# A fused attention and gated-MLP block on one core: the prologue's work is dealt out anew among the engines, and its order changed

## The chip, the cores and the metric

The kernel runs on one core of a Trainium2 chip. The metric is the device time of one execution in microseconds (us). Four compute engines take part: TensorE (PE in the profile), VectorE (DVE), ScalarE (ACT) and GpSimd (POOL); SyncE (SP) only issues DMAs. DMAs issued by SP run on a queue that the profile calls hardware_dynamic, those issued by GpSimd on one that it calls software_dynamic.

## The reference, cut to what matters

```python
# x: (1, 2048, 512); wqkv: (512, 1536); 32 heads of 16; F = 1792, Fh = 896
xn  = layernorm(x)                                  # eps 1e-5, no scale or shift
q, k, v = split_heads(xn @ wqkv)
A = softmax(q k^T / 4) v   ... @ wo                 # attention over all 2048 tokens
z = gelu(xn @ w_in);  z1 = z[..., :Fh];  z2 = layernorm(z[..., Fh:])
B = (z1 * (w_sp z2 + b_sp)) @ w_out                 # gMLP, w_sp mixes the 2048 tokens
out = x + A + B
```

All is fp32. The kernel gets fp32 accuracy from TensorE's fp32r format by splitting both operands of a product into a high part (rounded to fp32r) and a low part (what is left), and adding three products: high x high, low x high, high x low (`mm3`, lines 236 to 238).

## The kernel before, in words

**Tiling.** The 2048 tokens are 4 groups of 512, each of 4 tiles of 128 tokens. The width of 512 is 4 chunks of 128 (`ND` = 4). The 32 heads are taken in 16 pairs (`p`); q and k of four pairs come from one piece of weights, `m` = 0 to 3.

**Prologue** (before the line `steady.append(True)`). For each group g:

- `load_x(g)`: two DMAs by SP bring the group's tokens into the tiles `x{g}_0` and `x{g}_2`, two token tiles each.
- `norm_x(g)`: layernorm. DVE makes mean and variance of each tile (L318, L319), ACT the square root (L321), DVE the reciprocal and the shift (L322, L323), and then each tile of 128 x 512 is scaled and shifted in place (L327). With `parts` = 2 this goes by halves of two tiles. It is a generator, so its caller can run it in steps between other work.
- `turn_x(g)`: TensorE transposes the 16 blocks of 128 x 128 (L333), four to a PSUM bank; ACT copies each bank to the high half of `xnT{g}_{c}` (L71 in the profile, the line of the helper) and DVE subtracts to get the low half (L233).
- `qk_first(g)`: q and k of the first four head pairs for the group, each 12 matmuls of 128 x 512 (L236 to L238), then a split by ACT and DVE into the tile `qkhl`, and stores by SP to DRAM scratch (`qscr`, `kscr`): for q and for k one store of 512 KB and one of 256 KB.
- `load_stacks(0, ...)`: four loads of 96 KB by SP from that scratch into `qst0` and `kst0`, the stacked operands of the first head pair. SP works in order: a load that waits for its store to land holds what is queued behind it.
- `v_tile(t)`: V of one token tile, 12 matmuls (L236 to L238), evicted by ACT. Four of the 16 tiles (`EARLY` = 4) are done here, one a group; they use group 0's tokens. The weights of V (`wv0` to `wv3`) lie in `qst1` and `kst1`, which are free at that time.

Then `store(xscr[g][c], xnT[g, c])` writes the 16 tiles of the turned tokens, 512 KB each, to DRAM scratch, for the later work that reads them again. The code has these after the loop, and in the prologue `store` issues on GpSimd's queue (L155).

**Weights.** `begin` loads a piece of weights by SP in raw fp32; with `early` given, a second DMA, by GpSimd (L253), loads the same bytes straight into the high half (so that no copy is needed), and `end` then subtracts on DVE (L259). Without `early`, `end` lets GpSimd copy (L261) and subtract (L262). In the steady part other weights are split by GpSimd in the same way (L282, L284).

**Constants.** `cscr` is a row of ones in DRAM; `init_rows(a)` copies it to four rows of `kst[a]`, which carry the softmax shift into the scores' product. `init_rows(0)` belongs to the prologue and `init_rows(1)` to the first third of the first head pairs' work. `braw` and `bhl` hold the spatial bias `b_sp`.

**Order of the work.** Everything is written out in program order (`manual_schedule`): each engine takes its instructions in the order in which the code issues them, and waits by semaphores for operands and free buffers. After the prologue a planner, with costs and due times written in the code, interleaves the scores and their maxima (L1109 before the change), the dense products of the rest of V, q, k and the MLP (L1154), the scores for the softmax (L1095) and the products with V (L1192). After the prologue TensorE's first work is 48 dense matmuls for the next V tiles, and then the first maxima: products of `kst0` and `qst0`, of which the fourth pair of products needs the fourth group's k. DVE reduces them (L811).

Of the kernel before, what the change touches and what calls it, by code (L numbers as in the profile page):

```python
# [16 lines left out]
P = 128  # L17
# [36 lines left out]
def fused_block(ctx, tc, x, wqkv, wo, w_in, w_spT, b_sp, w_out, out):  # L54
# [66 lines left out]
    def raw(t):  # L121
        return t.bitcast(F32) if t.dtype == F32R else t

    def move(dst, src):
        nc.sync.dma_start(raw(dst), raw(src))
# [93 lines left out]
    def t512(nm):  # L219
        return big.tile([P, 512], F32, tag="t512", name=nm, bufs=4)  # L220
# [86 lines left out]
    def norm_x(g, parts=1):  # L307


        mv = sm.tile([P, 4, 2], F32, tag="mv", name=f"mv{g}", bufs=2)  # L310
        rs = sm.tile([P, 2, 4], F32, tag="rs", name=f"rs{g}", bufs=2)
        k = 4 // parts
        for a in range(parts):
            tiles = range(a * k, (a + 1) * k)
            sl = slice(a * k, (a + 1) * k)
            for i in tiles:
                st = sm.tile([P, 6], F32, tag="bst", name=f"bst{g}_{i}", bufs=4)
                nc.vector.bn_stats(st, xs[g, i])  # L318
                nc.vector.bn_aggr(mv[:, i, :], st)  # L319
            yield  # L320
            nc.scalar.activation(rs[:, 0, sl], mv[:, sl, 1], AF.Sqrt, bias=epst)  # L321
            nc.vector.reciprocal(rs[:, 0, sl], rs[:, 0, sl])  # L322
            nc.vector.scalar_tensor_tensor(rs[:, 1, sl], mv[:, sl, 0], -1.0, rs[:, 0, sl], ALU.mult, ALU.mult)  # L323
            for i in tiles:
                if i % 4 == 2:
                    yield
                nc.scalar.activation(xs[g, i], xs[g, i], AF.Identity, bias=rs[:, 1, i:i + 1], scale=rs[:, 0, i:i + 1])  # L327

    def turn_x(g):
        for c in range(ND):  # L330
# [635 lines left out]
        for _ in gen:  # L966
            pass

    def init_rows(a):

        for j in range(2):
            row = 64 * j + KS
            for r in range(2):
                nc.gpsimd.dma_start(raw(kst[a])[row + r:row + r + 1, :], cscr[0:1, :])

    engines = {mybir.EngineType.PE, mybir.EngineType.Activation, mybir.EngineType.DVE, mybir.EngineType.Pool, mybir.EngineType.SP}
    with tc.manual_schedule(engines=engines):
        load_x(0)
        w0 = [piece(f"wqk0_{a}") for a in range(2)]
        w0r = [begin(*qk_weights(0, a), early=w0[a]) for a in range(2)]  # L980
        load_x(1)
        ones = t512("ones")
        nc.vector.memset(ones[0:32, 0:P], 1.0)
        wv, wvr = [], []
        for c in range(ND):
            t = (qst, kst)[c // 2][1].rearrange("p (b a f) -> p b a f", b=2, a=2)[:, c % 2]
            wv.append(t)
            wvr.append(begin(f"wv{c}", wqkv[c * P:(c + 1) * P, 2 * D:3 * D], 512, early=t))
        nc.gpsimd.dma_start(cscr.rearrange("o (a b) -> (o a) b", b=P), ones[0:16, 0:P])
        nc.gpsimd.memset(vhead[:, :, :, DH:], 1.0)  # L990
        nc.gpsimd.memset(vall[:, NT * H * (DH + 1):], 0.0)
        for r in (0, 64):
            nc.vector.tensor_copy(onesr[r:r + 2, :], ones[0:2, 0:P])
        run(norm_x(0, 2))
        load_x(2)
        for r, t in zip(w0r, w0):
            end(r, t, True)
        turn_x(0)
        load_x(3)
        init_rows(0)  # L1000
        for r, t in zip(wvr, wv):
            end(r, t, True)
        norm = norm_x(1, 2)
        for g in range(NG):
            for _ in qk_first(g, w0):
                if g == 0:
                    next(norm, 0)
            load_stacks(0, slice(g * 512, (g + 1) * 512))
            for t in range(EARLY * g // NG, EARLY * (g + 1) // NG):
                v_tile(t, wv)  # L1010
            if g + 1 < NG:
                for _ in norm:
                    pass
                turn_x(g + 1)
                if g + 2 < NG:
                    norm = norm_x(g + 2)
                    next(norm)
        for g in range(NG):
            for c in range(ND):
                store(xscr[g][c], xnT[g, c])  # L1020
        steady.append(True)
        braw = t512("braw")[0:16, 0:P]
        bhl = hilo("bhl")[0:16, :, 0:P]
        move(braw, b_sp)
        nc.vector.tensor_copy(bhl[:, 0, :], braw)
        nc.vector.tensor_sub(bhl[:, 1, :], braw, bhl[:, 0, :].bitcast(F32))
        for a in range(2):
            move(bsplit[a:a + 1, :], bhl[:, a, :])
        T.update(P=0.0, A=0.0, D=0.0, G=0.0)
        room["big"] = RING - 16 + EARLY  # L1030
        prepare(wq, [((m, a), *qk_weights(m, a)) for m in (1, 2, 3) for a in range(2)])
# [50 lines left out]
        def scores():  # L1082
            nonlocal n_st
            p, c, kt = order[n_st]
            if n_st == 22:
                init_rows(1)
            i = n_st % 64
            if p + 1 < NP and stacks[0] <= p and i >= (3 if p else 20) and (not owed[0] or i >= LATE):
                stacks[0] = p + 1
                load_stacks(p + 1)  # L1090
            turn_to("R")
            k = take("s")
            for j in range(2):
                rows = slice(64 * j, 64 * j + KS + 2)
                nc.tensor.matmul(sl[k][:, j, :], kst[p % 2][rows, kt * P:(kt + 1) * P], qst[p % 2][rows, c * 512:(c + 1) * 512], start=True, stop=True)  # L1095
            T["P"] += SLOT
            spawn(exp(n_st, k), 1, T["P"] + 0.22)
            stpos[n_st] = pe
            n_st += 1
# [203 lines left out]
```

## Time and profile before

| | |
|---|---|
| time before, median of 3 runs | 1884.51 us (1882.85 to 1885.61) |
| the profiled execution's own time | 1888.93 us |
| its span in the trace | 1887.1 us |
| mean granted TensorE clock | 0.989 |
| TensorE busy | 1825.1 us of the span (97%) |
| VectorE, ScalarE, GpSimd busy | 1444.7, 1225.3, 690.7 us |
| TensorE's first matmul, first one after the prologue | 8.06, 74.40 us |

Times in rows of the trace are microseconds from the start of the span. A row of the timeline reads: start, length, engine, line, operation, out<-in, count, and in brackets the idle time before it with what ended it. A row of a group reads: line, engine, operation, names, shapes, count, then busy time and mean of one in ns, then idle time before and what ended it. Engine names with a q (SPq) are the engine's DMA issues.

### The profile page before, as it was taken

What the parts mean: (1) busy time and instruction counts of PE and PEld (TensorE: products, weight loads), DVE (VectorE), ACT (ScalarE), POOL (GpSimd) and SP (SyncE); (2) the same over time, 40 slices, a digit from 0 to 9 for tenths busy, and PEclk for the clock granted to TensorE, in tenths of its full rate; (3) what the DMA queues carried; (4) which work ended last, traced back from release to release, by engine and by line L of the source; (5) the groups of instructions that cost most, each with busy time, mean ns of one, the idle gap of its engine ahead of it and who ended that gap; (6) DMA issues with size and microseconds to landing.
All of it is one profiled execution on the core that took longest, in us unless ns stands there. A gap on an engine that the chain in (4) does not pass through costs nothing.

```text
span 1887.1 us, 38105 instructions
## 1 busy us (share of the span) xinstructions
PE 1825.1 (97%) x14812; PEld 1109.3 (59%) x14812; DVE 1444.7 (77%) x1677; ACT 1225.3 (65%) x1338; POOL 690.7 (37%) x797
## 2 busy tenths in 40 slices
PE   6899999999998999999999999999999999999998
PEld 5665656566554656566655656565656565556554
DVE  5577878888876878778777877787778777878873
ACT  4247777888775777666656666666666665656555
POOL 2202142687886878800171217000722140002110
PEclk9899999999998999999999999999999999999999
DMA  9505573444455353474677657463787576456342
GB/s 329 208 3 170 203 225 111 98 137 118 133 160 160 129 130 110 141 167 119 158 201 194 165 142 227 133 148 103 219 194 160 161 201 145 124 140 174 116 129 92
DMA packets 208109, 291.47 MB, mean 154 GB/s; under 512 B 36008, under 2 KB 107368, under 8 KB 205048
## 3 DMA queue, kind: packets, MB, share of 16 engines
q1 hardware_dynamic: 197944, 258.03, 50.6%
q0 software_dynamic: 9984, 31.01, 4.8%
q8 instruction: 116, 1.90, 0.4%
q14 instruction: 65, 0.53, 0.1%
HBM read 186.98 MB, written 101.98 MB: 153 GB/s over the span
## 4 chain that ended last, share of the span: by engine, by line
PE 84%; DMA 4%; DVE 4%; POOL 4%; issue 2%; ACT 2%; SPq 0%; DVEq 0%; POOLq 0%; ACTq 0%
PE dps L1154 33%; PE sl L1192 22%; PE sl L1095 13%; PE sl L1109 12%; DVE mm L811 3%; DMA mscr<-ms 1%; PE dps L1168 1%; POOL wsp L284 1%; ACT pf L71 1%; DMA wqk<-in_wqkv 1%; PE sl L236 0%; PE sl L237 0%; DMA qst<-mscr 0%; PE sl L238 0%; ACT x L327 0%
## 5 line engine op out<-in xcount | busy, mean ns | idle before, releaser
L811 DVE TENSOR_REDUCE mm<-sl 128x2 f32<-128x1024 f32 x1024 | 1226.2, 1223 | 184.0 <-PE sl L1109 178.3
L71 ACT ACTIVATE pf<-sl 128x1024 f32<-128x1024 f32 x1024 | 1042.9, 1027 | 356.6 <-PE sl L1095 315.4
L1192 PE MATMUL sl<-pf,vall 128*32 128x512 f32 x4096 | 467.3, 597 | 0.0
L1095 PE MATMUL sl<-qst,kst 50*128 50x512 f32 x2048 | 441.4, 421 | 13.0 <-DVE mm L811 2.9
L1154 PE MATMUL dps<-wsp,zs 64*128 64x512 f32 x2688 | 441.4, 393 | 3.1 <-DMA zs<-z2scr 3.1
L1109 PE MATMUL sl<-kst,qst 48*128 48x512 f32 x2048 | 428.1, 408 | 7.2 <-DVE mm L811 3.5
L1095 PEld LDWEIGHTS sl<-qst,kst 50*128 50x128 f32 x2048 | 197.6, 185 | 223.8 <-issue 85.7
L1154 PEld LDWEIGHTS dps<-wsp,zs 64*128 64x128 f32 x2688 | 266.8, 187 | 41.5 <-DMA zs<-z2scr 3.7
L1192 PEld LDWEIGHTS sl<-pf,vall 128*32 128x32 f32 x4096 | 120.3, 110 | 270.6 <-issue 241.1
L1109 PEld LDWEIGHTS sl<-kst,qst 48*128 48x128 f32 x2048 | 197.6, 186 | 113.5 <-ACT pf L71 54.6
L1212 DVE TENSOR_TENSOR e<-sl,e 128x512 f32<-128x512 f32 x64 | 44.3, 692 | 174.3 <-PE sl L1192 133.8
L720 POOL TENSOR_TENSOR hhl<-z1i,hhl 128x512 fp32r<-128x512 f32 x28 | 35.8, 1290 | 332.3 <-ACT hhl L71 332.3
L71 ACT ACTIVATE e<-sl 128x512 f32<-128x512 f32 x64 | 38.3, 599 | 176.5 <-PE sl L1192 159.9
L1154 PE MATMUL dps<-w,xt 64*128 64x448 f32 x768 | 110.9, 369 | 2.3 <-ACT z L71 0.4
L1154 PE MATMUL dps<-wout,hp 64*128 64x512 f32 x672 | 111.5, 393 | 0.0
L858 POOL TENSOR_TENSOR ob<-ob 128x512 f32<-128x512 f32 (+1 forms) x16 | 20.6, 1288 | 181.9 <-DMA ob<-rscr 181.9
L1154 PEld LDWEIGHTS dps<-w,xt 64*128 64x128 f32 x768 | 73.9, 186 | 17.1 <-issue 8.0
L420 POOL TENSOR_TENSOR qkhl<-qr,qkhl 128x512 fp32r<-128x512 f32 x24 | 30.4, 1285 | 115.2 <-ACT qkhl L71 93.7
L1154 PEld LDWEIGHTS dps<-wout,hp 64*128 64x128 f32 x672 | 65.5, 187 | 9.1
L854 POOL TENSOR_TENSOR ob<-ob 128x512 f32<-128x512 f32 (+1 forms) x16 | 21.0, 1312 | 96.8 <-DMA ob<-escr 96.8
L1154 PE MATMUL dps<-xnT,wqk 64*128 64x512 f32 x288 | 47.4, 396 | 1.1 <-ACT vall L71 0.4
L1154 PE MATMUL dps<-wo,op 64*128 64x512 f32 x288 | 47.5, 407 | 0.6
(279 smaller groups left out, 1629.0 us busy)
## 6 DMA issues: line engine op xcount, KB each, us to landing
zs<-z2scr SPq DMA_DIRECT2D x192, 256.0 KB
escr<-e SPq DMA_DIRECT2D x60, 256.0 KB
hscr<-hhl POOLq DMA_DIRECT2D x28, 512.0 KB, 5.6
qst<-qscr SPq DMA_DIRECT2D x30, 384.0 KB
kst<-kscr SPq DMA_DIRECT2D x30, 384.0 KB
qscr<-qkhl SPq DMA_DIRECT2D x16, 512.0 KB
xscr<-xnT POOLq DMA_DIRECT2D x16, 512.0 KB, 4.5
kscr<-qkhl SPq DMA_DIRECT2D x16, 512.0 KB
```

The source lines that it names most:

```text
L71: return nc.scalar.activation(out, in_, func, **kw)
L284: nc.gpsimd.tensor_sub(t[:, 1, :n], rw, t[:, 0, :n].bitcast(F32))
L420: nc.gpsimd.tensor_sub(hl[:, 1, :], raw_, hl[:, 0, :].bitcast(F32))
L720: nc.gpsimd.tensor_sub(hl[:, 1, :], z1, hl[:, 0, :].bitcast(F32))
L811: nc.vector.tensor_reduce(mmax[g][:, :, t, kc], sl[k], AX.X, ALU.max)
L854: nc.gpsimd.tensor_add(both_[rows, 0, :], both_[rows, 0, :], both_[rows, 1, :])
L858: nc.gpsimd.tensor_mul(both_[rows, 0, :], both_[rows, 0, :], both_[rows, 1, :])
L1095: nc.tensor.matmul(sl[k][:, j, :], kst[p % 2][rows, kt * P:(kt + 1) * P], qst[p % 2][rows, c * 512:(c + 1) * 512], start=True, stop=True)
L1109: nc.tensor.matmul(sl[k][:, j, :], qst[p % 2][rows, tt * P:(tt + 1) * P], kst[p % 2][rows, kc * 512:(kc + 1) * 512], start=True, stop=True)
L1154: nc.tensor.matmul(dps[:, bank, :w], lhs, rhs, start=go, stop=stop)
L1192: nc.tensor.matmul(sl[k][cols:cols + VW, 0, :], vpack(kt + r, 2 * p + j), pf[:, j * 512:(j + 1) * 512], start=n == n_pv, stop=n == n_pv + ...
L1212: nc.vector.tensor_add(e, sl[k][:, 0, :], e)
```

## The change

- In `norm_x` the scaling of the tokens (L327) goes from ACT to GpSimd, as one `tensor_scalar` with two per-partition operands.
- V's weights are no longer loaded twice: GpSimd's four early DMAs go, and GpSimd copies and subtracts instead (L261, L262); DVE's four subtractions (L259) go.
- The order of the prologue: group g + 1 is turned, and group g + 2 normalized, straight after group g's q and k; V's tiles come behind that, none with group 0, tile 0 with group 1, tiles 1 and 2 with group 2, tile 3 with group 3. All of group 2's tokens are loaded ahead of V's weights. The weights of q and k get their low halves after group 0 is turned, not before.
- Constants: the store to `cscr`, the rows of `kst[0]` and (later, in the steady part) of `kst[1]` go through SP's queue instead of GpSimd's; `braw` is loaded, and the bias split and stored, in the prologue instead of after it.

```diff
@@ -324,7 +324,7 @@
             for i in tiles:
                 if i % 4 == 2:
                     yield
-                nc.scalar.activation(xs[g, i], xs[g, i], AF.Identity, bias=rs[:, 1, i:i + 1], scale=rs[:, 0, i:i + 1])
+                nc.gpsimd.tensor_scalar(xs[g, i], xs[g, i], rs[:, 0, i:i + 1], rs[:, 1, i:i + 1], ALU.mult, ALU.add)
 
     def turn_x(g):
         for c in range(ND):
@@ -966,12 +966,11 @@
         for _ in gen:
             pass
 
-    def init_rows(a):
-
+    def init_rows(a, put):
         for j in range(2):
             row = 64 * j + KS
             for r in range(2):
-                nc.gpsimd.dma_start(raw(kst[a])[row + r:row + r + 1, :], cscr[0:1, :])
+                put(kst[a][row + r:row + r + 1, :], cscr[0:1, :])
 
     engines = {mybir.EngineType.PE, mybir.EngineType.Activation, mybir.EngineType.DVE, mybir.EngineType.Pool, mybir.EngineType.SP}
     with tc.manual_schedule(engines=engines):
@@ -979,53 +978,47 @@
         w0 = [piece(f"wqk0_{a}") for a in range(2)]
         w0r = [begin(*qk_weights(0, a), early=w0[a]) for a in range(2)]
         load_x(1)
+        load_x(2)
         ones = t512("ones")
         nc.vector.memset(ones[0:32, 0:P], 1.0)
-        wv, wvr = [], []
-        for c in range(ND):
-            t = (qst, kst)[c // 2][1].rearrange("p (b a f) -> p b a f", b=2, a=2)[:, c % 2]
-            wv.append(t)
-            wvr.append(begin(f"wv{c}", wqkv[c * P:(c + 1) * P, 2 * D:3 * D], 512, early=t))
-        nc.gpsimd.dma_start(cscr.rearrange("o (a b) -> (o a) b", b=P), ones[0:16, 0:P])
-        nc.gpsimd.memset(vhead[:, :, :, DH:], 1.0)
-        nc.gpsimd.memset(vall[:, NT * H * (DH + 1):], 0.0)
+        move(cscr.rearrange("o (a b) -> (o a) b", b=P), ones[0:16, 0:P])
+        wv = [(qst, kst)[c // 2][1].rearrange("p (b a f) -> p b a f", b=2, a=2)[:, c % 2] for c in range(ND)]
+        wvr = [begin(f"wv{c}", wqkv[c * P:(c + 1) * P, 2 * D:3 * D], 512) for c in range(ND)]
+        load_x(3)
+        braw = t512("braw")[0:16, 0:P]
+        bhl = hilo("bhl")[0:16, :, 0:P]
+        move(braw, b_sp)
+        init_rows(0, move)
         for r in (0, 64):
             nc.vector.tensor_copy(onesr[r:r + 2, :], ones[0:2, 0:P])
         run(norm_x(0, 2))
-        load_x(2)
+        turn_x(0)
         for r, t in zip(w0r, w0):
             end(r, t, True)
-        turn_x(0)
-        load_x(3)
-        init_rows(0)
-        for r, t in zip(wvr, wv):
-            end(r, t, True)
-        norm = norm_x(1, 2)
+        run(norm_x(1, 2))
+        nc.gpsimd.memset(vhead[:, :, :, DH:], 1.0)
+        nc.gpsimd.memset(vall[:, NT * H * (DH + 1):], 0.0)
         for g in range(NG):
-            for _ in qk_first(g, w0):
-                if g == 0:
-                    next(norm, 0)
+            run(qk_first(g, w0))
             load_stacks(0, slice(g * 512, (g + 1) * 512))
-            for t in range(EARLY * g // NG, EARLY * (g + 1) // NG):
+            if g == 0:
+                nc.vector.tensor_copy(bhl[:, 0, :], braw)
+                nc.vector.tensor_sub(bhl[:, 1, :], braw, bhl[:, 0, :].bitcast(F32))
+                for a in range(2):
+                    move(bsplit[a:a + 1, :], bhl[:, a, :])
+            if g + 1 < NG:
+                turn_x(g + 1)
+            if g + 2 < NG:
+                run(norm_x(g + 2, 2))
+            if g == 0:
+                for r, t in zip(wvr, wv):
+                    end(r, t)
+            for t in ((), (0,), (1, 2), (3,))[g]:
                 v_tile(t, wv)
-            if g + 1 < NG:
-                for _ in norm:
-                    pass
-                turn_x(g + 1)
-                if g + 2 < NG:
-                    norm = norm_x(g + 2)
-                    next(norm)
         for g in range(NG):
             for c in range(ND):
                 store(xscr[g][c], xnT[g, c])
         steady.append(True)
-        braw = t512("braw")[0:16, 0:P]
-        bhl = hilo("bhl")[0:16, :, 0:P]
-        move(braw, b_sp)
-        nc.vector.tensor_copy(bhl[:, 0, :], braw)
-        nc.vector.tensor_sub(bhl[:, 1, :], braw, bhl[:, 0, :].bitcast(F32))
-        for a in range(2):
-            move(bsplit[a:a + 1, :], bhl[:, a, :])
         T.update(P=0.0, A=0.0, D=0.0, G=0.0)
         room["big"] = RING - 16 + EARLY
         prepare(wq, [((m, a), *qk_weights(m, a)) for m in (1, 2, 3) for a in range(2)])
@@ -1083,7 +1076,7 @@
             nonlocal n_st
             p, c, kt = order[n_st]
             if n_st == 22:
-                init_rows(1)
+                init_rows(1, move)
             i = n_st % 64
             if p + 1 < NP and stacks[0] <= p and i >= (3 if p else 20) and (not owed[0] or i >= LATE):
                 stacks[0] = p + 1
```

The code after the prologue is the same but for `init_rows(1, move)`. Its line numbers are 7 lower (L1109 is L1102 after the change, L1154 is L1147, L811 is the same).

What the change does to the engines' order, at two places.

**TensorE, where group 0's q and k end.** Names: `xnT0_3` is the fourth chunk of group 0's turned tokens, `wqk0_1` the weights of k, `kst1` holds V's weights, `x1_0` and `x1_2` are the tokens of group 1, `ident` the identity for a transpose. Before:

```order
L238 MATMUL sl1_187<-xnT0_3_281,wqk0_1_196 128x512
L236 MATMUL sl2_188<-qst1_91,xnT0_0_260 128x512
L237 MATMUL sl2_188<-qst1_91,xnT0_0_260 128x512
...
L237 MATMUL sl2_188<-kst1_93,xnT0_3_281 128x512
L238 MATMUL sl2_188<-kst1_93,xnT0_3_281 128x512
L333 MATMUL dps_185<-ident_72,x1_0_203 128x128 x2
L333 MATMUL dps_185<-ident_72,x1_2_204 128x128 x2
```

After:

```order
L238 MATMUL sl1_187<-xnT0_3_284,wqk0_1_196 128x512
L333 MATMUL sl2_188<-ident_72,x1_0_203 128x128 x2
L333 MATMUL sl2_188<-ident_72,x1_2_204 128x128 x2
L333 MATMUL dps_185<-ident_72,x1_0_203 128x128 x2
L333 MATMUL dps_185<-ident_72,x1_2_204 128x128 x2
...
L333 MATMUL sl1_187<-ident_72,x1_2_204 128x128 x2
L236 MATMUL sl2_188<-xnT1_0_361,wqk0_0_195 128x512
```

V's first tile stood between group 0's q and k and the transposes of group 1; now the transposes follow at once. For the whole prologue the order of TensorE's blocks was q/k 0, V 0, turn 1, q/k 1, V 1, turn 2, q/k 2, V 2, turn 3, q/k 3, V 3, and is now q/k 0, turn 1, q/k 1, turn 2, V 0, q/k 2, turn 3, V 1, V 2, q/k 3, V 3.

**GpSimd, ahead of the stores of the turned tokens.** Names: `cscr` to `kst0` are the constant rows, `xscr0_0<-xnT0_0` is the store of the first chunk of group 0, `wv2r` and `wv3r` are raw pieces of V's weights, `x3_0` and `x3_2` the tokens of group 3. Before:

```order
L253 DMA qst1_91<-in_wqkv 128x512 x2
L253 DMA kst1_93<-in_wqkv 128x512 x2
L989 DMA cscr_168<-ones_207 16x128
L990 MEMSET vall_87 128x512
L991 MEMSET vall_87 128x15
L974 DMA kst0_92<-cscr_168 1x16x128 x4
L155 DMA xscr0_0_102<-xnT0_0_260 128x1024
L155 DMA xscr0_1_103<-xnT0_1_267 128x1024
L155 DMA xscr0_2_104<-xnT0_2_274 128x1024
L155 DMA xscr0_3_105<-xnT0_3_281 128x1024
L155 DMA xscr1_0_106<-xnT1_0_375 128x1024
```

After:

```order
L327 TENSOR_SCALAR x2_2_208<-x2_2_208,rs2_386 128x512 x2
L261 CAST qst1_91<-wv0r_214 128x512
L262 TENSOR_TENSOR qst1_91<-wv0r_214,qst1_91 128x512
...
L261 CAST kst1_93<-wv3r_220 128x512
L262 TENSOR_TENSOR kst1_93<-wv3r_220,kst1_93 128x512
L327 TENSOR_SCALAR x3_0_222<-x3_0_222,rs3_484 128x512 x2
L327 TENSOR_SCALAR x3_2_223<-x3_2_223,rs3_484 128x512 x2
L155 DMA xscr0_0_102<-xnT0_0_263 128x1024
L155 DMA xscr0_1_103<-xnT0_1_270 128x1024
```

GpSimd had nothing but small work ahead of the first store and between the stores of one group and the next; now all tokens' scaling and V's weights stand ahead of the first store, and the 16 stores follow one another.

## The prediction

> **What bounds the kernel now.** I begin with the page: the span, the busy times, and the chain of work that ended last.
>
> ```profile
> span 1887.1 us, 38105 instructions
> PE 1825.1 (97%) x14812; PEld 1109.3 (59%) x14812; DVE 1444.7 (77%) x1677; ACT 1225.3 (65%) x1338; POOL 690.7 (37%) x797
> PE 84%; DMA 4%; DVE 4%; POOL 4%; issue 2%; ACT 2%; SPq 0%; DVEq 0%; POOLq 0%; ACTq 0%
> ```
>
> TensorE sets the end. Its order of work after the prologue is the same before and after, so the change can be worth only what it takes from, or adds to, TensorE's time up to the place where its rows meet no new wait. The table by stage splits the span at 74.40 us, where the prologue's last matmul gives way to the dense work; columns are stretch, length, then busy time of PE and the other engines, at the end granted clock, DMA share and GB/s.
>
> ```profile
> 0.00:74.40 74.40, 54.40 (x208) 42.75 (x208) 35.29 (x81) 31.07 (x51) 17.24 (x37) 0.89 0.87 308
> 106.00:1887.10 1781.10, 1741.34 (x14370) 1043.89 (x14366) 1384.62 (x1569) 1190.96 (x1281) 662.29 (x748) 0.99 0.55 149
> ```
>
> In the prologue TensorE is idle for 74.40 - 54.40 = 20.0 us, and its clock is 0.89 where later it is 0.99. But the DMA share there is 0.87, so a shorter prologue runs into the transfers. The waits up to 110 us say what TensorE waited for (total, times, longest):
>
> ```profile
> POOL xscr L155 <- DVE xnT L233: 35.8, 10, 13.5
> PE sl L333 <- ACT x L327: 15.7, 12, 8.1
> ```
>
> The transposes wait for scaled tokens: 15.7 us, of which 8.1 are the start. The stores of turned tokens wait for nothing but their tiles, so they leave spread out, group by group. TensorE's timeline gives the marks:
>
> ```profile
> 22.69 0.39 PE L236 MATMUL sl<-qst,xnT 128*128 128x512 f32 x1
> 30.75 0.77 PE L236 MATMUL dps<-xnT,wqk 128*128 128x512 f32 x1
> 42.32 0.33 PE L333 MATMUL sl<-ident,x 128*128 128x128 f32 x1 [2.13 <-ACT x L327]
> 44.43 0.48 PE L333 MATMUL sl<-ident,x 128*128 128x128 f32 x1 [0.23 <-ACT x L327]
> 47.12 0.78 PE L236 MATMUL sl<-xnT,wqk 128*128 128x512 f32 x1
> 49.83 0.43 PE L236 MATMUL sl<-xnT,wqk 128*128 128x512 f32 x1
> 50.09 0.39 PE L237 MATMUL sl<-xnT,wqk 128*128 128x512 f32 x1
> 53.95 0.39 PE L236 MATMUL sl<-qst,xnT 128*128 128x512 f32 x1
> 74.40 1.65 PE L1154 MATMUL dps<-qst,xnT 64*128 64x512 f32 x12 [0.69 <-ACT vall L71]
> 80.33 0.88 PE L1109 MATMUL sl<-kst,qst 48*128 48x512 f32 x6
> 82.95 0.40 PE L1109 MATMUL sl<-kst,qst 48*128 48x512 f32 x2
> ```
>
> Group 0's q and k end at 22.69 and group 1's begin at 30.75; V's first tile and a turn lie between. From 50.09 to 53.95 run 17 matmuls, 0.227 us each: 24 of them (q and k) are 5.45 us, a V tile of 12 is 2.72. From 47.12 to 49.83 six take 2.71, 0.45 each: after the wait of 2.13 at 42.32 TensorE runs at half speed until 49.83, which costs half of 2.71 = 1.4 us, counted from 44.43 half of 5.4 = 2.7. The row at 82.95 is the fourth pair of maxima, 8.55 us behind the start of the dense work; it needs the fourth group's k.
>
> **The change part by part.** The prices on the other engines, from the groups by shape and the timelines:
>
> ```profile
> L523 POOL TENSOR_SCALAR z<-z,zrs 128x512 f32<-128x512 f32 x16 | 12.4, 774 | 10.3 <-ACT z2hl L71 10.2
> L327 ACT ACTIVATE x<-x,rs 128x512 f32<-128x512 f32 x16 | 11.9, 804 | 3.0 <-DVE rs L323 3.0
> L282 POOL CAST wqk<-wqk_0r 128x512 fp32r<-128x512 f32 x3 | 1.8, 609 | 17.9 <-DMA wqk_0r<-in_wqkv 17.8
> L284 POOL TENSOR_TENSOR wqk<-wqk_1r,wqk 128x512 fp32r<-128x512 f32 x3 | 3.9, 1287 | 0.1
> 7.03 0.69 DVE L318 BATCH_NORM_STATS2 bst<-x 128x6 f32<-128x512 f32 x1
> 9.28 0.16 DVE L323 SCALAR_TENSOR_TENSOR rs<-mv,rs 128x2 f32<-128x2 f32 x1
> 30.30 1.30 DVE L233 TENSOR_TENSOR xnT<-sl,xnT 128x512 fp32r<-128x512 f32 x2
> ```
>
> L523 is the same operation as the new L327: multiply and add with two per-partition operands, on 128 x 512. So a tile's scaling costs 0.774 us on GpSimd for 0.804 on ACT.
>
> *Group 0.* 4 x 0.03 us less. The first product could start sooner, since DVE now splits the tokens before it makes the weights' low halves; but the second product of each three needs such a half, and both pieces of DVE work stand ahead of it as before: 22.7 stays, within 0.3. V's early loads, 1 MB, leave the transfers of the start, where from then on no engine on the path waits for one.
>
> *Group 1.* Its tokens are scaled while q and k of group 0 run, so it is turned at once. The turn at 42.32 took 4.80 (to 47.12) with waits; with none I take 16 blocks in 3.1. Group 1's q and k begin at 25.8, 4.95 earlier, and end at 25.8 + 5.45 = 31.3, on a warm clock. V's first tile is moved behind, not saved.
>
> *Group 2.* Its statistics stand on DVE behind group 1's splits, four of 0.65 (30.30), from 25 to about 27.3. Half a group takes 9.44 - 7.03 = 2.41. Two halves, 32.1, and two scalings, 1.55: 33.7. TensorE waits 2.4 us; the turn ends near 36.3.
>
> *V's weights.* They stand on GpSimd behind group 2's scaling: four times 0.609 + 1.287 = 1.90, 7.6 us, to 41.3; V's first tile ends at 42.0, where it would have ended at 36.3 + 2.7 = 39.0. This costs 3.0 us: the early loads had hidden it before.
>
> *The rest.* q and k 2 to 48 (5.45 and some half speed); group 3's scaling is done at 41.3 + 4 x 0.774 = 44.4, so its turn doesn't wait: 51.1; two V tiles 56.6; q and k 3 62.0; V 3 64.8; the dense work starts 0.7 later at **65.5 instead of 74.40, 8.9 us sooner**. Bounds from the uncertain steps (a scaling as dear as the 1.287 row, no half speed) are 64 to 67.
>
> *What is late next.* Three views of the transfers: the issues of SP, the queues in two windows, and the sizes.
>
> ```profile
> 24.24 1.73 SPq L125 DMA_DIRECT2D kscr<-qkhl  x2
> 72.43 0.88 SPq L125 DMA_DIRECT2D kscr<-qkhl  x2
> 77.24 0.41 SPq L125 DMA_DIRECT2D kst<-kscr  x1
> q0 software_dynamic: 384, 1.44, 101.6%
> q1 hardware_dynamic: 13, 0.02, 1.3%
> q0 software_dynamic: 142, 0.52, 66.4%
> q1 hardware_dynamic: 129, 0.26, 34.7%
> xscr<-xnT POOLq DMA_DIRECT2D x16, 512.0 KB, 4.5
> qscr<-qkhl SPq DMA_DIRECT2D x1, 512.0 KB
> qscr<-qkhl SPq DMA_DIRECT2D x1, 256.0 KB
> qst<-qscr SPq DMA_DIRECT2D x2, 96.0 KB
> ```
>
> The first pair of queue rows is the window 24.8 to 28.4: group 0's four stores move 1.44 MB, 0.40 a microsecond, while the k stores that SP issued at 24.24 stand still. The second pair is 28.4 to 30.4: packet for packet, so the smaller packets of SP's queue get a third, 0.13 MB a microsecond. After the change all 16 stores stand behind group 3's scaling and go out from 44.4: 8.39 MB in one stretch. In the same stretch fall q and k of groups 2 and 3: for each 2 x (512 + 256) KB stored and 4 x 96 KB loaded, 1.92 MB by these rows' units, 3.8 for both. Together 12.3 MB at 0.40 from about 46.5: 31 us, to 77. SP's share alone says the same: 1.92 MB at 0.13 are 14.8 us a group, so group 2 from 46.5 to 61 and group 3 to 76. With the last loads' latency (before, from the issue at 77.24, some 2 us) k of group 3 lands near **79.5**, hardly sooner than before, though its matmuls end 10 us sooner.
>
> TensorE reaches the fourth maxima at 65.5 + 8.55 = 74.05 and waits 5.5 us for that. It goes on at 79.5 instead of 82.95, 3.45 sooner, and the wait cools the clock: 1.4 to 2.7 us at the rows above, I take 2.2, since the wait is longer than theirs. **Net: 3.45 - 2.2 = 1.2 us saved.**
>
> [...]
>
> *Moved, hidden.* `init_rows(1)` leaves GpSimd for SP:
>
> ```profile
> 129.73 1.98 POOL L974 DMA_DIRECT2D kst<-cscr  x4 [33.97 <-PE sl L1095]
> 153.04 2.73 POOL L420 TENSOR_TENSOR qkhl<-qr,qkhl 128x512 fp32r<-128x512 f32 x2 [21.33 <-DMA qst<-qscr]
> ```
>
> GpSimd idles on both sides, so nothing is gained; on SP four more issues of about 0.4 are hidden in its idle time, 0 to 1.6 if not. The bias and the first constant rows go into the prologue, on engines that wait there: nothing. ACT loses 16 scalings (11.9 us), none with TensorE behind it.
>
> The profiled execution gives 1888.93 - 1.2 = 1887.7. It lies 4.42 above the median of the runs shown, which I forecast: 1884.51 - 1.2 = **1883.3 us**. A measurement of this kernel can tell about 0.2%, 3.8 us, so this is no change that can be told.
>
> **The rivals.**
>
> *Faster: SP's queue isn't held up.* The row at 72.43 to the end near 79.4 is a chain of 7 us without competing stores. If group 3's q and k get through as then (k stored at 62.6, landed near 70), nothing waits at 74.05, and the gain is the 8.9 of the dense work's start, less 1 to 2 for odd waits: 1876 to 1878. The wide DMA share (0.87) and the window 24.8 to 28.4 speak against it; for it speaks that SP gets equal turns once started, and that software stores landed in 4.5 us.
>
> *Faster by less: the landing is right and the clock isn't cooled,* or the stores drain at 76: gain 3.5 to 6, 1879 to 1881.
>
> *Slower: GpSimd becomes the bound.* Each microsecond that its chain (scaling, V's weights, scaling) is later, the stores begin later, and, since the transfers are one stretch, the landing too. If a scaling takes 1.29 like the subtraction's row, that is 12 x 0.5 = 6 us up to the first store, part of it on the path of groups 1 and 2 as well: landing at 84 to 85, TensorE 2 to 3 later than before and a cooling on top: 1887 to 1890. It turns to slower from 1.2 us of delay, and to what can be told from 5. [...] No run here shows the scaling beside VectorE's statistics; by the L523 row, taken while VectorE reduced maxima, it isn't dearer.
>
> *It does nothing:* the turn ahead of q and k waits as before. The order excludes it for group 1.
>
> **How the numbers follow.** Forecast (gain or loss within 3.8): 0.43. SP's queue unhindered: 0.20. Partly: 0.12 beyond 0.2%. Slower by GpSimd's chain: 0.25. Its own range is 1880 to 1887; to leave out 2 in 10 it must reach into both sides: 1877 to 1889. Faster 0.32, same 0.43, slower 0.25.
>
> **What would show it.** TensorE: qk 1 from 25.8, the wait at group 2 near 31 to 34, V's first tile spread by GpSimd to 42, dense work from 64 to 67. The queues: software stores in one block from 44 to 77, SP's rows at a third beside it, the last `kst<-kscr` landing at 79 to 80, and a wait of 4 to 7 us ahead of the fourth maxima (L1102 after the change) with a half clock behind it. A dense start earlier than 64 or later than 67 breaks the order of steps; a landing at 70 to 74 breaks the step on the queues; a later first store than 45 gives the slower rival.

## The result, and the profile after

The change makes the kernel a little slower. The median of 18 runs after the change is 1888.86 us (1882.38 to 1891.95), that of 18 runs of the kernel before 1885.7 us (1882.85 to 1890.16); the ratio is 1.0012, with a 95% interval of 1.0003 to 1.002, which is 0.6 to 3.8 us. The forecast was 1.2 us faster; the sign was wrong.

The table by stage of the changed kernel (columns as in the prediction):

```profile
0.00:74.40 74.40, 54.50 (x272) 41.01 (x272) 38.08 (x86) 20.14 (x39) 32.01 (x52) 1.00 0.83 293
74.40:106.00 31.60, 23.91 (x168) 17.59 (x170) 20.59 (x23) 2.17 (x4) 11.11 (x12) 0.84 0.26 78
```

By 74.40 us TensorE has done 272 matmuls (208 before), at a granted clock of 1.00 (0.89 before; 0.95 in a second profile of the changed kernel). In the next 31.6 us it does only 168 (238 before), at a clock of 0.84 (1.00 before). What the prologue won is gone by 106 us. TensorE's timeline of the changed kernel shows where:

```profile
25.02 0.50 PE L236 MATMUL sl<-xnT,wqk 128*128 128x512 f32 x1 [0.31 <-DVE xnT L233]
32.41 0.33 PE L333 MATMUL sl<-ident,x 128*128 128x128 f32 x1 [1.25 <-POOL x L327]
63.44 1.65 PE L1147 MATMUL dps<-qst,xnT 64*128 64x512 f32 x12 [0.69 <-ACT vall L71]
80.07 0.76 PE L1102 MATMUL sl<-kst,qst 48*128 48x512 f32 x1 [7.90 <-DMA kst<-kscr]
81.18 0.79 PE L1102 MATMUL sl<-kst,qst 48*128 48x512 f32 x1 [0.34 <-DMA kst<-kscr]
86.05 0.63 PE L1102 MATMUL sl<-kst,qst 48*128 48x512 f32 x2
87.53 0.40 PE L1102 MATMUL sl<-kst,qst 48*128 48x512 f32 x2
```

The dense work starts at 63.44 instead of 74.40. The fourth pair of maxima is two matmuls, one on each half of k's rows, and each half comes by a load of its own from `kscr` to `kst`. The first waits 7.90 us for the fourth group's k and goes on at 80.07; the second starts at 81.18. Before the change the two start together, at 82.95. Then the matmuls of 512 columns take 0.76 where later they take 0.40; the table gives the clock (columns as above), which is 0.50 up to 86.7 and 1.00 from there:

```profile
80.00:86.00 6.00, 5.51 (x20) 3.58 (x22) 2.45 (x2) 0.00 (x0) 3.23 (x4) 0.50 0.65 184
76.50:86.70 10.20, 6.21 (x24) 4.14 (x26) 2.45 (x2) 0.00 (x0) 3.93 (x5) 0.50 0.49 143
86.75:100.00 13.25, 11.74 (x96) 8.84 (x96) 12.89 (x12) 2.17 (x4) 7.12 (x8) 1.00 0.14 41
```

On GpSimd, the last scaling, the stores, and the last of the 16 stores:

```profile
40.74 3.02 POOL L327 TENSOR_SCALAR x<-x,rs 128x512 f32<-128x512 f32 x4
43.70 4.84 POOL L155 DMA_DIRECT2D xscr<-xnT  x9
61.98 0.53 POOL L155 DMA_DIRECT2D xscr<-xnT  x1 [1.10 <-DMA xscr<-xnT]
```

The stores leave in a block from 43.70. Nine go at once; from then on each waits for an earlier one to land. On SP's queue, in the same stretch:

```profile
48.21 1.87 SPq L125 DMA_DIRECT2D kscr<-qkhl  x2
...
60.81 0.32 SPq L125 DMA_DIRECT2D kst<-kscr  x1
...
62.50 1.24 SPq L125 DMA_DIRECT2D kst<-kscr  x1
63.79 2.80 SPq L125 DMA_DIRECT2D qscr<-qkhl  x2
66.64 2.76 SPq L125 DMA_DIRECT2D kscr<-qkhl  x2
...
78.58 0.41 SPq L125 DMA_DIRECT2D kst<-kscr  x1
```

Group 2's k is stored at 48.21 and its first load can only be issued at 60.81, when the store has landed: 12.6 us, where in the kernel before the same step for group 3 took 76.09 - 72.43 = 3.7. Group 3's q and k, split by 61.4, stand behind it in SP's order: their stores are issued at 63.79 and 66.64. The two queues, first from 52 to 56, then from 60 to 64 us (packets, MB, share of the DMA engines):

```profile
q0 software_dynamic: 287, 1.04, 67.6%
q1 hardware_dynamic: 276, 0.53, 35.2%
```

```profile
q0 software_dynamic: 453, 1.63, 100.4%
q1 hardware_dynamic: 34, 0.04, 2.7%
```

From 52 to 56 it is one packet for one (287 to 276), so SP gets a third by bytes. From 60 to 64 SP's queue moves only 0.04 MB, though SP issues three loads from 60.81 on.

### The profile page after: what moved, and what is told of

It is laid out like the page before. It is cut to its first block, busy times and chain, and to the rows that moved or that the text cites. A ratio compares the mean times of both kernels' runs of the same rounds, so it can differ in the third digit from the quotient of the medians.

```text
span 1887.4 us, 38112 instructions
## 1 busy us (share of the span) xinstructions
PE 1820.6 (96%) x14812; PEld 1098.9 (58%) x14812; DVE 1443.8 (76%) x1677; ACT 1212.5 (64%) x1324; POOL 702.1 (37%) x808
## 4 chain that ended last, share of the span: by engine, by line
PE 86%; DVE 4%; POOL 3%; DMA 2%; issue 2%; ACT 1%; SPq 1%; DVEq 0%; POOLq 0%; ACTq 0%
PE dps L1147 35%; PE sl L1185 23%; PE sl L1088 13%; PE sl L1102 12%; DVE mm L811 3%; DMA kscr<-qkhl 1%; PE dps L1161 1%; ACT pf L71 1%; SPq L125 1%; POOL w L284 0%; POOL z2hl L525 0%; DMA wsp_12r<-in_w_spT 0%; DVE bst L318 0%; ACT vall L71 0%; DMA ob<-rscr 0%
## 5 line engine op out<-in xcount | busy, mean ns | idle before, releaser
L811 DVE TENSOR_REDUCE mm<-sl 128x2 f32<-128x1024 f32 x1024 | 1226.2, 1222 | 203.1 <-PE sl L1102 198.0
L1102 PE MATMUL sl<-kst,qst 48*128 48x512 f32 x2048 | 429.0, 409 | 15.5 <-DMA kst<-kscr 8.2
L1147 PE MATMUL dps<-wsp,zs 64*128 64x512 f32 x2688 | 441.4, 394 | 1.9 <-DMA zs<-z2scr 1.9
L1147 PEld LDWEIGHTS dps<-wsp,zs 64*128 64x128 f32 x2688 | 265.9, 188 | 41.4 <-DMA zs<-z2scr 2.8
L1102 PEld LDWEIGHTS sl<-kst,qst 48*128 48x128 f32 x2048 | 198.3, 186 | 123.4 <-ACT pf L71 57.6
L1147 PE MATMUL dps<-w,xt 64*128 64x448 f32 x768 | 110.6, 369 | 2.3 <-ACT z L71 0.4
L1147 PE MATMUL dps<-wout,hp 64*128 64x512 f32 x672 | 111.3, 392 | 0.0
L1147 PEld LDWEIGHTS dps<-w,xt 64*128 64x128 f32 x768 | 73.3, 186 | 17.7 <-issue 8.1
L1147 PEld LDWEIGHTS dps<-wout,hp 64*128 64x128 f32 x672 | 65.4, 187 | 8.9
L1147 PE MATMUL dps<-xnT,wqk 64*128 64x512 f32 x288 | 47.3, 396 | 1.1 <-ACT vall L71 0.4
L1147 PE MATMUL dps<-wo,op 64*128 64x512 f32 x288 | 46.1, 397 | 0.6
```

The costliest lines, as they stand in the source:

```text
L811: nc.vector.tensor_reduce(mmax[g][:, :, t, kc], sl[k], AX.X, ALU.max)
L1102: nc.tensor.matmul(sl[k][:, j, :], qst[p % 2][rows, tt * P:(tt + 1) * P], kst[p % 2][rows, kc * 512:(kc + 1) * 512], start=True, stop=True)
L1147: nc.tensor.matmul(dps[:, bank, :w], lhs, rhs, start=go, stop=stop)
```

## The experiments

Theory A: the block of stores, which GpSimd's new work puts off, holds SP's queue, the fourth group's k lands at 80 to 81 wherever its matmuls end, and TensorE pays the wait and a cooled clock. Theory B: the k is late because of all the prologue's transfers together, or of SP's order alone. All diffs below are against the changed kernel unless another is named. A mark is used throughout: the start of DVE's maxima number 20 (counted from 0), the first row of this kind behind 104 us in the kernel before:

```profile
105.27 2.36 DVE L811 TENSOR_REDUCE mm<-sl 128x2 f32<-128x1024 f32 x2 [0.72 <-PE sl L1109]
```

**The stores spread among the groups** (e1_spread):

```diff
+    def keep(g):
+        for c in range(ND):
+            store(xscr[g][c], xnT[g, c])
...
         nc.gpsimd.memset(vall[:, NT * H * (DH + 1):], 0.0)
+        keep(0)
...
                 turn_x(g + 1)
+            if g == 0:
+                keep(1)
...
                     end(r, t)
+            elif g + 1 < NG:
+                keep(g + 1)
...
-        for g in range(NG):
-            for c in range(ND):
-                store(xscr[g][c], xnT[g, c])
```

> The change, with the 16 stores of turned tokens put back among the groups: group 0's behind group 1's scaling, group 1's ahead of group 2's scaling, group 2's behind group 3's scaling, group 3's when it is turned. Theory A (the block of stores behind GpSimd's work holds SP's queue at a third and less, and so delays the fourth group's k): half of the 8.39 MB has left by about 36 us, the dense work starts at 62 to 65 as after the change, the last k load lands near 68 to 71, no wait ahead of the fourth maxima, which stand at 71 to 74 instead of 80.07 (82.95 before): 1875 to 1878, ratio to before 0.994 to 0.996. Theory B (the k is late because the prologue's transfers are too many in all, or because SP's own chain in order is too long, wherever the stores stand): a wait of 5 us and more stays, within 2 us of the changed kernel's 1888.9.

Measured: 1878.65 us, ratio to before 0.9964 (0.995 to 0.9977), 6.8 us faster than the kernel before. Its stores on GpSimd, then TensorE's dense start and fourth maxima:

```profile
23.76 4.28 POOL L155 DMA_DIRECT2D xscr<-xnT  x8
44.07 2.19 POOL L155 DMA_DIRECT2D xscr<-xnT  x4
50.25 2.33 POOL L155 DMA_DIRECT2D xscr<-xnT  x4 [3.99 <-DVE xnT L233]
```

```profile
64.63 1.66 PE L1153 MATMUL dps<-qst,xnT 64*128 64x512 f32 x12 [0.69 <-ACT vall L71]
73.20 0.40 PE L1108 MATMUL sl<-kst,qst 48*128 48x512 f32 x2
```

No wait at the fourth maxima, full speed, the mark at 95.49. The bytes are the same, so theory B falls: their place counts. The last load of `kst`, issued at 69.05, is in time, as A has it. The time is just above A's 1875 to 1878.

**The scaling back on ACT** (e2_act):

```diff
-                nc.gpsimd.tensor_scalar(xs[g, i], xs[g, i], rs[:, 0, i:i + 1], rs[:, 1, i:i + 1], ALU.mult, ALU.add)
+                nc.scalar.activation(xs[g, i], xs[g, i], AF.Identity, bias=rs[:, 1, i:i + 1], scale=rs[:, 0, i:i + 1])
```

> The change, with the scaling of the tokens put back on ACT, and nothing else undone. Theory A: GpSimd then splits V's weights when they land (by about 28 us) and has nothing else ahead of the stores; groups 0 and 1 leave by 33, group 2 near 37, group 3 near 50, without a block at the end; dense work from 61 to 65, last k load at 68 to 72, wait ahead of the fourth maxima under 2 us: 1875 to 1879. Theory B (the block isn't caused by GpSimd's scaling, or the transfers are too many in all): the wait of 5 us and more stays, 1886 to 1890.

Measured: 1885.87 us, ratio 1.0005 (0.9994 to 1.0015): theory A's number missed by 7 us. Its stores on GpSimd and two of its waits (total, times, longest) say why:

```profile
24.18 2.18 POOL L155 DMA_DIRECT2D xscr<-xnT  x4
27.09 2.33 POOL L155 DMA_DIRECT2D xscr<-xnT  x4 [0.72 <-DVE xnT L233]
```

```profile
ACT qkhl L71 <- DMA kscr<-qkhl: 5.2, 1, 5.2
PE dps L333 <- DVE qkhl L233: 5.2, 1, 5.2
```

The block was gone from the end, as A has it, but eight stores left at 24 to 29. Beside them a store to `kscr` landed late, ACT waited 5.2 us for its buffer `qkhl`, and TensorE waited 5.2 us behind ACT in the middle of turning group 2. Its dense work started at 70.22. So the same contention took another victim. The time is within 0.2 of theory B's 1886 to 1890, but B's sign is not there: the fourth maxima stand at 78.78, without a wait of 5 us. That the stall is the stores' doing, and not ACT's, was then only argued; the last experiment tests it.

**The stores behind the fourth group's k** (e3_late):

```diff
+        held_ = sm.tile([P, 4], F32, tag="held", name="held", bufs=1)
+        for r in (0, 64):
+            nc.gpsimd.tensor_copy(held_[r:r + KS], raw(kst[0])[r:r + KS, S - 4:S])
         for g in range(NG):
             for c in range(ND):
                 store(xscr[g][c], xnT[g, c])
```

> The change, with the 16 stores still in one block at the end of GpSimd's work, but behind two tiny GpSimd copies (48 x 4 each) that read the last columns of the fourth group's k in kst0, so that no store leaves before that k has landed. Theory A: SP's queue is alone, group 3's k is stored at 61 and lands at 67 to 70, no wait ahead of the fourth maxima (71 to 74), and the stores run from 68 to 90 beside the first weights of the steady part, which come later by up to 10 us (first read of the stored tokens is at 185.8, so nothing waits for them): 1875 to 1879, unless the late weights make a wait of their own. Theory B (too long a chain on SP by itself): the wait of 5 us stays.

Measured: 1878.41 us, ratio 0.9966 (0.9954 to 0.9977). The first stores and the fourth maxima in this kernel:

```profile
69.89 4.32 POOL L155 DMA_DIRECT2D xscr<-xnT  x8 [0.32 <-issue]
```

```profile
72.75 0.40 PE L1105 MATMUL sl<-kst,qst 48*128 48x512 f32 x2
```

The block is whole, only later, and costs nothing there: SP's chain by itself is short enough. Theory B falls for its second half too.

**The clock's price, first try** (e4_warm):

```diff
             k = take("m")
+            if n_mx == 3:
+                for _ in range(32):
+                    nc.tensor.matmul(sl[k][:, 0, :], qst[0][0:KS, 0:P], kst[0][0:KS, 0:512], start=True, stop=True)
```

> The change, with 32 matmuls more on TensorE ahead of the fourth maxima: they read columns of qst0 and kst0 that landed long before, and write the bank that the fourth maxima then overwrite. 32 x 0.227 = 7.3 us of the 7.9 that TensorE waits there. The stores are untouched, so the last k loads land at 80 to 81 in every theory. Theory A (the cooled clock after the wait costs half of the 6 us from 80.07 to 86.05, 3 us): the clock stays whole, the place that stood 0.7 behind the kernel before at 106 us stands 2 to 2.5 ahead of it, 1885 to 1887, 2 to 3 less than the changed kernel in the same rounds. Theory B (the cooling costs nothing that isn't made up later): as the changed kernel, within 1 us.

Measured: 1890.53 us, ratio 1.0034 (1.0024 to 1.0044): a miss on both theories. The profiled execution was the longest of the twelve, 1900.09. In its timeline and table by stage:

```profile
74.27 0.79 PE L1105 MATMUL sl<-kst,qst 48*128 48x512 f32 x1 [3.20 <-DMA kst<-kscr]
74.28 2.92 PE L1150 MATMUL dps<-qst,xnT 64*128 64x512 f32 x10
76.58 13.00 PE L1102 MATMUL sl<-kst,qst 48*128 48x512 f32 x30
```

```profile
76.60:89.00 12.40, 12.40 (x34) 9.51 (x31) 0.00 (x0) 0.00 (x0) 5.68 (x7) 0.50 0.45 132
```

In this execution an earlier load of k was late too (3.20 us), the clock was down before the extra matmuls began (the ten dense ones at 74.28 took 2.92 us, where ten take 1.43 at 70.75 in the changed kernel), and 12.4 us without a gap of matmuls on 48 rows did not bring it back: it was 0.50 over them. The extra work ran at half speed, 0.43 us each, past the landing (the last load of k was issued at 78.90). It settles nothing about the price.

**Profiles of the unchanged kernels** (p1_before, p2_before, p3_after). What was open: the two first profiles differ by 0.7 us at the mark, the medians by 3.2.

> The kernel before, unchanged, for a second profile: what is open is that the changed kernel stood 0.7 us behind the kernel before at 106 us and 0.3 at the end in the two profiles, and 2 to 3 us behind in the medians of 18 runs. Theory T1 (the clock's windows fall differently in each execution, so that the first profile of the kernel before had a dear prologue): the mark where DVE's maxima number 20 starts, at 105.27 in the first profile, stands at 102 to 104. Theory T2 (the prologue is the same each time, and the missing 2 us are lost later): it stands within 0.3 of 105.27, and the rest differs.

> The kernel before, unchanged, for a third profile; as for the second: T1 102 to 104 at maxima number 20, T2 within 0.3 of 105.27.

> The changed kernel, unchanged, for a second profile: the wait ahead of the fourth maxima again, 7 to 9 us, k landing at 79 to 83 (the stores' block decides it in every theory). T1: maxima number 20, at 105.95 in its first profile, moves by 1 to 3 us with the clock. T2: within 0.5 of 105.95.

Measured, with the fourth maxima and the mark read from TensorE's and DVE's timelines as above:

| kernel, profile | dense start | fourth maxima | mark | from one to the other |
|---|---|---|---|---|
| before, first | 74.40 | 82.95 | 105.27 | 22.32 |
| before, second | 72.41 | 80.96 | 103.31 | 22.35 |
| before, third | 73.88 | 82.43 | 104.77 | 22.34 |
| after, first | 63.44 | 80.07 | 105.95 | 25.88 |
| after, second | 64.09 | 80.75 | 105.96 | 25.21 |

Neither theory as put: one profile of the kernel before fits T1, the other lies between. The changed kernel's mark moved by 0.01, as T2 has it. Together they show that the prologue of the kernel before varies by 2 us, and that its first profile was the dearest of three. On the means, the fourth maxima come 82.11 - 80.41 = 1.7 us sooner after the change, the stretch behind them is 25.55 - 22.34 = 3.2 us longer, and the mark is 105.96 - 104.45 = 1.5 us later, inside the 0.6 to 3.8 of the runs.

The table counts from the first of the two matmuls. In the second profile, as in the first, the other one comes later, and the clock is at half up to 85.5:

```profile
80.75 0.76 PE L1102 MATMUL sl<-kst,qst 48*128 48x512 f32 x1 [7.94 <-DMA kst<-kscr]
81.88 0.79 PE L1102 MATMUL sl<-kst,qst 48*128 48x512 f32 x1 [0.38 <-DMA kst<-kscr]
```

```profile
75.40:85.50 10.10, 4.38 (x18) 3.12 (x18) 1.88 (x2) 0.00 (x0) 2.13 (x3) 0.50 0.60 179
```

From the second matmul (81.18 and 81.88, mean 81.53) to the mark it is 24.77 and 24.08 us, 2.4 and 1.7 more than the 22.34 before, 2.1 on the mean. So of the 3.2 us, 1.1 lie between the two matmuls, and 2.1 behind them, where the clock is at half.

**Dense work in the place of the wait** (e5_fill), and as its control the same in the kernel before (e8_before_fill):

```diff
-FIRST = 7.0
+FIRST = 17.0
```

> The change, with the planner's start of the maxima set from 7 to 17 of its time units, so that TensorE does some 40 dense matmuls more ahead of the first maxima; the stores in a block are untouched, so the fourth group's k lands at 79 to 82 as in the changed kernel. Theory A (what the block costs is the wait and the cooled clock at the fourth maxima, and nothing else): the wait is 0 to 3 us instead of 7.9 and the clock stays whole, dense work that was due later stands in its place, 1879 to 1883, some 6 to 9 us less than the changed kernel, less what the other order of the rest costs. Theory B (the dense work moved ahead is missing later, or the block costs through late weights): within 2 us of the changed kernel.

> The kernel before with the maxima started at 17 instead of 7 units, a control for the experiment that did this to the changed kernel and gained 5 us on the kernel before. The kernel before has no wait at the fourth maxima. Theory A for that experiment (it took away the wait): no gain here, 1883 to 1887. The rival (the other order of the body is what gained, above all the clock's stretch at half speed near 565 us, which was absent there): 1876 to 1880 here too.

Measured: 1878.85 us, ratio 0.9971 (0.996 to 0.9981), in the changed kernel; 1886.94 us, ratio 1.0006 (0.9997 to 1.0015), in the kernel before. The last load of k and the fourth maxima in the first of the two:

```profile
80.01 0.41 SPq L125 DMA_DIRECT2D kst<-kscr  x1
```

```profile
84.50 0.39 PE L1102 MATMUL sl<-kst,qst 48*128 48x512 f32 x2
```

The k lands as late as in the changed kernel, and nobody waits: dense work stands there, the maxima come behind it at full speed. The rival, that another order of the body gains, is answered by the control, which has that order and gains nothing. The difference between the two is there from the start: DVE's maxima number 20 begin at 106.55 in the changed kernel and at 114.84 in the control.

**Both remedies** (e6_spread_fill: the first experiment and `FIRST = 17.0`).

> The stores spread among the groups (as in the first experiment) and the maxima started at 17 instead of 7 of the planner's units. If the two gains are of one cause (the wait at the fourth maxima), there is nothing left for the later start to win: 1877 to 1880, as either alone. If what the later start won lies elsewhere (another order of the body), the gains add up: 1868 to 1873.

Measured: 1878.64 us, ratio 0.9963 (0.9951 to 0.9975). No sum: the two take away the same cost.

**The clock's price, second try** (e7_warm128): the 32 matmuls of 128 rows.

```diff
+            if n_mx == 3:
+                for _ in range(32):
+                    nc.tensor.matmul(sl[k][:, 0, :], xnT[3, 1][:, 0, 0:P], xnT[3, 0][:, 0, :], start=True, stop=True)
```

> The changed kernel with 32 matmuls more ahead of the fourth maxima, as in the fourth experiment, but of 128 rows by 128 columns (the turned tokens of group 3 with themselves) instead of 48 rows. Theory A (the clock went down because nothing but waits and 48-row work stood there, and costs 2.5 to 3 us): the 32 run at 0.227 us, the wait that is left is under 1.5 us, the fourth maxima resume at 80 to 82 at full speed, maxima number 20 at 103 to 104 instead of 106.0, the time 2 to 3 us less than the changed kernel's. Theory B (the clock goes down whatever TensorE does there): the 32 run at about 0.43 from some point, and it is slower than the changed kernel.

Measured: 1889.63 us, ratio 1.0023 (1.0014 to 1.0033). As a remedy it failed: TensorE came to that place later in this execution, and nothing waits behind the extra work, which ended at 85. TensorE was at half speed just before it, with 2.66 us for ten dense matmuls where the changed kernel's ten at 70.75 took 1.43, but over the extra work the clock was 0.93, and from 85 to 106 it was 1.00 (timeline, then table by stage):

```profile
74.40 2.66 PE L1150 MATMUL dps<-qst,xnT 64*128 64x512 f32 x10
76.99 8.09 PE L1102 MATMUL sl<-xnT,xnT 128*128 128x512 f32 x32
85.01 0.50 PE L1105 MATMUL sl<-kst,qst 48*128 48x512 f32 x2
```

```profile
77.00:85.00 8.00, 8.00 (x33) 6.34 (x32) 0.00 (x0) 0.00 (x0) 0.99 (x2) 0.93 0.63 181
```

The 32 take 0.25 us each. If the clock changed once in these 8.00 us, from 0.50 to 1.00, the 0.93 puts that some 1.1 us into them, at 78.1 (an estimate). The mark is at 107.41, 22.40 behind its fourth maxima, as in the three profiles before (22.3), not 25.2 to 25.9 as after the change. With a whole clock and the two matmuls of the fourth maxima together, the stretch is as long as before the change; this agrees with the split of the 3.2 us above.

**The fourth corner** (e9_act_late: the stores behind the k, and the scaling on ACT; both diffs above).

> The stores behind the fourth group's k (as in the third experiment), and the tokens scaled on ACT again (as in the second): the fourth corner of the square. In the second experiment ACT stood 5.2 us ahead of group 1's k, because its buffer's store to kscr had not landed beside the eight stores that left at 24 to 29. Theory A (that is the stores' doing too): without stores the stall is gone, V's weights are split on GpSimd before V's first tile needs them, the dense work starts at 61.5 to 63.5 (64.2 with GpSimd's scaling), no wait at the fourth maxima, 1875 to 1878. Rival (ACT's scaling itself holds ACT's copies, whatever the stores do): dense work at 66 and later, 1880 to 1884.

Measured: 1876.31 us (before in the same rounds 1886.52), ratio 0.9946 (0.9932 to 0.9959). TensorE's dense start and fourth maxima:

```profile
62.85 1.65 PE L1150 MATMUL dps<-qst,xnT 64*128 64x512 f32 x12 [0.69 <-ACT vall L71]
71.40 0.40 PE L1105 MATMUL sl<-kst,qst 48*128 48x512 f32 x2
```

Theory A: without stores beside it, ACT's stall of 5.2 us is gone and the dense work starts 7.4 us sooner than in the second experiment. This version beats both kernels. Its interval overlaps that of the third experiment, so no gain from scaling on GpSimd is shown; the better figure is ACT's. The square of the four, as ratios to the kernel before:

| scaling | stores as in the change's order | stores behind the fourth group's k |
|---|---|---|
| on GpSimd | 1.0012 (stores issued from 43.7 to 62) | 0.9966 |
| on ACT | 1.0005 (24 to 58) | 0.9946 |

## Why the prediction was wrong

The mechanism was right: the block of stores, the late k, the wait, the half clock. The sum had the wrong sign, because its first term was some six times too large.

- *Groups 0 to 3 and V's weights.* Group 1's q and k began at 25.02 (25.8 forecast), group 2's tokens were scaled at 33.1 (33.7), V's weights split at 40.7 (41.3), group 3's tokens scaled at 43.7 (44.4). The scaling on GpSimd took 0.76 us a tile (0.774). The dense work began at 63.44 and 64.09, where 65.5 was forecast and 64 to 67 were its bounds; half a microsecond below the bound in one profile. Since TensorE waits at the fourth maxima, that was worth nothing.
- *What is late next.* The queue step held: stores from 43.7 in a block, a third of the bytes for SP, total rate 0.39 MB a microsecond (1.57 MB from 52 to 56) for 0.40. What it left out is the stretch from 60 to 64, in which SP's queue moved next to nothing, and that the two halves of k land one after the other.
- *The base.* The forecast took 82.95 for the kernel before, from the one profile at hand, the dearest of three; their mean is 82.11.
- **The step that failed: "It goes on at 79.5 instead of 82.95, 3.45 sooner", the first term of the net.** The forecast has one landing of k, near 79.5. TensorE had the first half at 80.07 and 80.75, but the second, without which the fourth maxima are not complete, at 81.18 and 81.88, on the mean 81.53, which is 2.0 later. Against the base of 82.11 that is 0.6 us sooner, not 3.45. The second term was right in size: 2.1 us for the cooled clock, where 2.2 was forecast. 0.6 - 2.1 is 1.5 us lost, the distance of the marks.
- *The clock.* In the two profiles the half clock cost 2.4 and 1.7 us. It was granted up to 86.7 in the first, 6.6 us after TensorE had gone on, and up to 85.5 at least in the second, 4.8 us after. That TensorE ran at half speed straight after the wait of 2.13 at 42.32, as the prediction has it for the kernel before, says too much: the transpose at 42.32, behind that wait, still took 0.33 us, and only the next, at 43.02, took 0.47. TensorE had then worked 0.33 us in the 2.8 since its last V matmul.
- *The rivals.* "SP's queue isn't held up" and "the clock isn't cooled" are refuted by the rows above. "GpSimd becomes the bound" had the sign, and its 1887 to 1890 holds the 1888.86, but by luck: GpSimd's chain was 0.7 us early, not late, and the scaling cost 0.76 us also where VectorE's statistics ran beside it (two tiles in 1.52 us from 29.25, statistics from 29.06 to 30.76). Without the block the prologue is worth 6 to 10 us, as the experiments show; the rival on SP's queue had priced that at 8.9 less 1 to 2.

What stays open: the first and third experiments are 9.0 and 9.4 us ahead at the mark, against the mean of the three profiles, and 6.8 and 6.4 in the ratios, whose intervals reach to 9.4 and 8.7. The second is 2.8 us ahead at the mark and not faster in the runs. Half-speed stretches of TensorE's clock in the body (the mean clock from 540 to 610 us is 0.85 to 0.90 in the five profiles of the unchanged kernels) vary by as much as the difference, but no run singles them out. The constants' move to SP's queue was not tried by itself; in the first pair of profiles maxima number 26 and number 65, at 113 and 183 us on either side of it, are both 0.7 us apart. Over the five profiles the changed kernel is on the mean 1.5 us behind at number 20, still 1.5 at number 100 (near 241 us), and about 3 at number 300 (near 601 us), past the half-speed stretch that begins near 565 (clock 0.50 from 565.4 to 578.9 in the first profile of the kernel before, from 564.7 to 581.0 in the first of the changed one). So the constants, moved at about 130 us, cost nothing that these profiles show.

## What to carry to other kernels

When work is moved onto an engine that also issues DMAs, list the issues that stand behind it: here 16 stores came later, in a block from 43.70, and what they then ran beside was the real price, a wait of 7.90 us for the fourth group's k. A store that nobody reads for 100 us belongs behind the transfers that somebody waits for; here two tiny copies ahead of the stores did it (1878.41 us for 1888.86). Where a result needs several loads, forecast each landing: here the second half of k, in use at 81.18, counted, not the first at 80.07. And where a forecast is the small difference of two larger terms, from one profile of a place that varies by 2 us, its sign is not known.

## What the runs showed of the hardware that was not expected

- At half clock, 12.4 us of gapless matmuls on 48 rows by 128 columns left the clock at 0.50 (e4_warm, 76.6 to 89.0). Over 8.00 us of matmuls on 128 rows it was 0.93 (e7_warm128; ten dense matmuls on 64 rows each, 2.66 us, ran just before them). In the kernel before, with transposes and matmuls on 128 rows from 43.02 on, it was 0.50 from 43.1 to 49.85 and 1.00 from 49.9 to 53. No run changes the rows alone, so it is not shown that they made the difference.
- In the changed kernel the half clock that begins in the wait at the fourth maxima was granted from 76.5 to 86.7 us in the first profile, and from 75.4 to 85.5 at least in the second. TensorE went on at 80.07 and 80.75, and the price was 2.4 and 1.7 us.
- In the changed kernel GpSimd issued nine stores of 512 KB, 4.84 us, without a wait (eight, 4.32 us, in e3_late); then each waited for a landing, 10.2 us in all over seven.
- Beside a backlog of GpSimd's stores, SP's queue, with loads newly issued at 60.81, moved 0.04 MB in 4 us (60 to 64); from 52 to 56 it had moved one packet for one.
